# Making the sums of w_out's blocks on VectorE alone, through three buffers in turn

## The chip, the core and the metric

The kernel runs on one core of one Trainium2 chip. Its time is the device time of one execution in microseconds (us). TensorE does the matmuls, VectorE (DVE), ScalarE (ACT) and GpSimd (POOL) the elementwise work, SyncE (SP) issues the transfers. Each engine works through its own list of instructions in the order in which the program holds them, and waits on semaphores for the others.

## What is computed

The reference is a chain of three parts over 2304 tokens: attention with a bias made by a small network from relative positions, a gated block, and a block with squared ReLU. The change lies in the last:

```python
def _moe2_ref(x, w_in, w_out):          # x 2304x512, w_in 512x2048, w_out 2048x512
    h = np.maximum(x @ w_in, 0.0)
    return (h * h @ w_out).astype(np.float32)
```

## The kernel before

Every f32 matrix product is made of three f16 ones: each operand is split into a high half and a low half (the rest), and high x high, high x low and low x high are summed in PSUM. `parts2` makes such a split: a cast for the high half (L1198 on VectorE, L1200 on ScalarE) and a subtraction for the low half (`diff`, L1193, on VectorE or GpSimd). Which engine takes which is set by the table `MIX`: each letter has a cycle of engines (0 VectorE, 1 GpSimd or ScalarE), and `mixed` takes the next one at each call.

The last block runs over nine units of 256 tokens. The first is taken alone, by `plain(0)`: for each f of 0 to 7, `layer1` makes two groups of 12 matmuls (L1375), ScalarE evacuates each (L1380, ReLU) and squares it (L1384) into `zx`, and `parts2` writes both halves of block f into a part of `wr`; then 96 matmuls (L1403) make the output, 48 for each half of the tokens, block after block. The other eight units are taken in four pairs. `hidden` does `layer1` for a pair and forms four sums and differences of quarters of the result on GpSimd (`zx<-zx`, L1193); `outputs` multiplies them in seven products instead of eight (a Winograd scheme, L1447), which needs the like sums of w_out's quarters on the other side. I call `plain(0)` the single unit and the four pairs the first to the last pair stage. PSUM for L1375 and L1403 comes from five buffers in turn.

Those sums of w_out's quarters are made once, by `combine(f)` for f of 0 to 7: three sums of 512 columns and four of 256, in f32, in the buffer `w2t` of 1024 columns, each from the last, and then one `parts2` of 1024 columns into `st["TS"][f]`. In the names of the trace these are `w2t<-w2r`, `w2t<-w2t,w2r` and `w2t<-w2r,w2t` for the sums, and `w2s`, `w2c`, `w2r` or `wr` `<-w2t` for the split. The seven sums take their engine from letter "t", (0, 0, 1): two on VectorE, one on GpSimd. `combine` for f of 0 to 2 is called in `weights2`, for 3 to 6 between the blocks of `plain`, and for 7 after them.

The engines' order isn't the order of the code: the program is built by a scheduler that models the engines' times and places each instruction when its inputs and its buffer are free by that model. So a sum that waits for the buffer `w2t` is placed later, among other work.

Of the kernel before, what the change touches and what calls it, by code (L numbers as in the profile page):

```python
# [10 lines left out]
F32 = mybir.dt.float32  # L11
# [13 lines left out]
P = 128  # L25
# [4 lines left out]
MIX = {  # L30
# [4 lines left out]
}  # L35

# [39 lines left out]
def tile_attention_moe(  # L76
# [25 lines left out]
    st = {}  # L102
# [3 lines left out]
    def keep(n=1):  # L106
        sc_n[0] += 1
        return res.tile([P, n], F32, name=f"keep{sc_n[0]}")
# [77 lines left out]
    def mul(out_, a, b, f=1.0):  # L186
        nc.vector.scalar_tensor_tensor(out=out_, in0=a, scalar=f, in1=b, op0=ALU.mult, op1=ALU.mult)
# [26 lines left out]
    def mixed(k):  # L214

        mix_n[k] = mix_n.get(k, -1) + 1
        return MIX[k][mix_n[k] % len(MIX[k])]
# [197 lines left out]
    def mm():  # L415
        return ps_mm.tile([P, 512], F32, tag="mm", name="mm", bufs=2)
# [775 lines left out]
    def diff(out_, a, b, how, op=ALU.subtract):  # L1192
        (nc.gpsimd if how else nc.vector).tensor_tensor(out=out_, in0=a, in1=b, op=op)  # L1193

    def parts2(hi, lo, x, hw, lw):
        how = mixed(hw)
        if how == 0:
            nc.vector.tensor_copy(hi, x)  # L1198
        elif how == 1:
            nc.scalar.copy(hi, x)  # L1200
        else:
            nc.gpsimd.tensor_scalar(
                out=hi, in0=x, scalar1=1.0, scalar2=0.0, op0=ALU.mult, op1=ALU.add)
        diff(lo, x, hi, mixed(lw))

    def combine(f):

        q = st["w2r"].t.rearrange("p a b -> p (a b)").bitcast(F16).rearrange("p (s c) -> p s c", c=256)
        t = st["w2t"]
        tv = t.rearrange("p (a b c) -> p a b c", a=2, b=2)  # L1210
        t1, t2, t3, t4 = [t[:, 256 * i:256 * i + 256] for i in range(4)]
        a, b = 4 * (W2 + f), 4 * (W2 + 8 + f)

        def right(l):
            return q[:, a + 2 * l + 1:b + 2 * l + 2:32, :]

        def left(l):
            return q[:, a + 2 * l:a + 2 * l + 2, :]

        t13 = tv[:, :, 0, :]  # L1220
        diff(t13, right(0), left(0), mixed("t"))
        diff(t13, t13, right(1), mixed("t"), ALU.add)
        diff(t13, t13, left(1), mixed("t"))
        for x, c, y in ((t2, b + 1, t1), (t4, b, t2)):
            diff(x, q[:, c], y, mixed("t"))
            diff(x, x, q[:, c + 2], mixed("t"), ALU.add)
        hi, lo = st["TS"][f]
        parts2(hi, lo, t, "c", "d")

    def yt_load(us):  # L1230
        n = 256 * len(us)
        yt = st["yt"][:, 0:8 * n].rearrange("p (l t) -> p l t", l=8)
        for i, u in enumerate(us):
            nc.sync.dma_start_transpose(out=yt[:, :, 256 * i:256 * i + 256], in_=y_d[u][:, :])

    def weights2():
        a_stack.close()
        w2p = ctx.enter_context(tc.tile_pool(name="w2p", bufs=2, side="right"))
        ps2 = ctx.enter_context(tc.tile_pool(name="ps2", bufs=5, space=PSUM))
        w2r = Ring(w2p.tile([P, 25, 512], F32, name="w2r", bufs=1), {  # L1240
            "w": lambda j, kc: (w2a, 4 * j + kc) if j < 2 else 4 * j - 8 + kc, "2": lambda j, kc: W2 + kc})
        st["w2p"], st["ps2"], st["w2r"] = w2p, ps2, w2r

        def mm2():
            return ps2.tile([P, 512], F32, tag="ph", name="mm2")

        w2s = w2p.tile([P, 3584], F32, name="w2s", bufs=1)
        sg2 = Stage(
            512, [w2s[:, 1024 * i:1024 * i + 1024].bitcast(I64) for i in range(3)],
            [w2s[:, 3072 + 256 * i:3328 + 256 * i].bitcast(BF16) for i in range(2)])  # L1250
        yield from first(w2r, {"w": w2i}, range(2, 4), block_rows, sg2, 3, mm2)
        kappa = []
        for j in range(4):
            kap = keep()
            mul(kap, st["iw", j], st["iw", j], KR)
            kappa.append(kap)
        yield from second(w2r, "2", NF2, w2o, kappa, sg2, 3, mm2, True)
        new = w2p.tile([P, 4096], F16, name="w2c", bufs=1)

        st["w2t"] = w2p.tile([P, 1024], F32, name="w2t", bufs=1)  # L1260
        w2h, wrh, w2sh = [t.rearrange("p a b -> p (a b)").bitcast(F16) for t in (
            w2r.t, wr.t, w2s.rearrange("p (a b) -> p a b", a=7))]
        rooms2 = [w2sh[:, 1024 * i:1024 * i + 1024] for i in range(7)] + [w2h[:, 1024 * 24:1024 * 25]] + [
            new[:, 1024 * i:1024 * i + 1024] for i in range(4)] + [
            wrh[:, 1024 * i:1024 * i + 1024] for i in (4, 5, 6, 36)]
        st["TS"] = [rooms2[2 * f:2 * f + 2] for f in range(8)]
        st["HS"] = [wrh[:, int(1024 * o):int(1024 * o) + 3584] for o in (7.5, 11, 15, 18.5, 22, 25.5, 29, 32.5)]
        st["yt"] = wrh[:, 0:4096]
        for f in range(3):
            if f == 1:  # L1270
                yield ("gv", 8)
                yt_load((0,))
            combine(f)
            yield 3.0
# [61 lines left out]
    w2p, ps2, w2r = st["w2p"], st["ps2"], st["w2r"]  # L1336

    def mm2():
        return ps2.tile([P, 512], F32, tag="ph", name="mm2")
# [5 lines left out]


    wk = ctx.enter_context(tc.tile_pool(name="wk", bufs=2, side="left"))
    fac = res.tile([P, 18], F32, name="fac")
    nc.vector.tensor_scalar(out=fac, in0=ftok, scalar1=st["G1"], scalar2=None, op0=ALU.mult)
    mul(fac, fac, fac)  # L1350
# [83 lines left out]
    def outputs(us):  # L1434
        n = 256 * len(us)
        nh = n // 2
        last_bank = mm2()
        for t in range(nh // P):
            banks = [mm2(), mm2(), mm2()] if t else [ma(), mm(), mm()]
            (p1, p2), (p6, p7), (p5, p3) = [[bk[:, 256 * i:256 * i + 256] for i in range(2)] for bk in banks]  # L1440
            p4 = last_bank[:, 256 * t:256 * t + 256]

            def product(po, a, b, fs=range(8)):
                for f in fs:
                    for k, (l, wl) in enumerate(((0, 0), (0, 1), (1, 0))):
                        o = nh * (a - 1 + 7 * l) + P * t
                        nc.tensor.matmul(  # L1447
                            po, HS[f][:, o:o + P], right_of(f, wl, b),
                            start=f == 0 and k == 0, stop=f == 7 and k == 2)

            def sums(name):
                return wk.tile([P, 256], F32, tag=name, name=name)

            def add(name, x, y):
                o = sums(name)
                nc.vector.tensor_tensor(out=o, in0=x, in1=y, op=ALU.add)
                return o

            def row(j, h, src, other):

                i = nh * (1 - h) + P * t
                u, tt = us[i // 256], i % 256 // P
                sc = fac[:, 2 * u + tt:2 * u + tt + 1]
                o = obs[h][:, 256 * j:256 * j + 256]
                nc.vector.tensor_tensor(out=o, in0=src, in1=other, op=ALU.add)
                nc.scalar.activation(o, o, AF.Copy, scale=sc)

            obs = [wk.tile([P, DM], F32, tag="ob", name="ob", bufs=3) for _ in range(2)]
            early_, late_ = (range(6), range(6, 8)) if t == 0 else (range(8), ())
            for fs in (early_, late_):  # L1470
                for po, a, b in ((p1, A11, B11), (p6, S2, T2), (p5, S1, T1)):
                    product(po, a, b, fs)
            c1 = sums("c1")
            nc.scalar.copy(c1, p1)
            u2 = add("u2", p6, c1)
            u4 = add("u4", p5, u2)
            product(p7, S3, T3)
            u3 = add("u3", p7, u2)
            row(1, 1, p5, u3)
            product(p2, A12, B21)  # L1480
            row(0, 0, p2, c1)
            product(p3, S4, B22)
            row(1, 0, p3, u4)
            product(p4, A22, T4)
            row(0, 1, p4, u3)
            for h in range(2):
                i = nh * (1 - h) + P * t
                for p0, np_, r0 in out_rows(us[i // 256], i % 256 // P):
                    nc.sync.dma_start(out[r0:r0 + np_, :], obs[h][p0:p0 + np_, :])
# [37 lines left out]
```

## Time and profile before

| | |
|---|---|
| three timed runs | 1247.25 us median, 1245.92 to 1251.09 |
| the profiled execution | 1241.6 us, span 1239.8 us |
| TensorE busy | 1099.7 us, 89% of the span |
| VectorE, ScalarE, GpSimd busy | 782.3, 669.9, 642.3 us |
| `plain(0)`, from its second group to its last matmul | 868.05 to 908.34 |
| first pair stage | 908.34 to 1001.18 |
| the other three | 1001.18 to 1079.30, 1157.42 and 1235.54 |

Times of rows are counted from the start of the span. A row of the order of time names an engine, a line, an operation, output<-input, shapes and a count; in brackets stands how long the engine stood idle ahead of it and what released it. The granted clock is a share of TensorE's full 2.4 GHz; 1.00 is all of it, and a mean in between mixes the two levels 1.2 and 2.4.

### The profile page before, as it was taken

Reading aid. Unit: us, or ns where it says so; the run is one execution under the profiler, and the core shown is the slowest. Engines: PE = TensorE matmul, PEld = TensorE weight load, DVE = VectorE, ACT = ScalarE, POOL = GpSimd, SP = SyncE. Lnnn points to the kernel's source line nnn. Section 1 sums busy time; section 2 is a strip of 40 time slices with the busy share of each in tenths; the row PEclk is TensorE's granted clock in tenths of the full one; section 3 lists DMA queues with packets and bytes.
Section 4 is the critical chain, followed back from the end, with each engine's and each line's share of the span. In section 5 each row is a group of like instructions: output and inputs, shape, how many; then the busy total and the mean of one; then the engine's idle time right before and its main releaser. Section 6 shows DMA issues by size and latency. Waiting matters only on the chain. (4 is left out here: it accounts for less than half of the span.)

```text
span 1239.8 us, 27146 instructions
## 1 busy us (share of the span) xinstructions
PE 1099.7 (89%) x10478; PEld 811.3 (65%) x10478; DVE 782.3 (63%) x1866; ACT 669.9 (54%) x1350; POOL 642.3 (52%) x811
## 2 busy tenths in 40 slices
PE   2587799998678889999997999979998899999998
PEld 2566788686467578686774767556743756848657
DVE  5989857887676666666565745884757335153361
ACT  3567767557566566566563543365635245163451
POOL 2433213279768697778694462235567236062360
PEclk9779799999879999999999999989999899999999
DMA  8957543219999999998989994650201101002001
GB/s 220 266 134 208 177 132 87 50 58 201 220 214 209 217 218 169 230 184 170 182 170 247 240 228 129 213 176 10 43 17 23 30 18 35 35 1 52 19 1 35
DMA packets 278078, 163.20 MB, mean 132 GB/s; under 512 B 233276, under 2 KB 246588, under 8 KB 277948
## 3 DMA queue, kind: packets, MB, share of 16 engines
q1 hardware_dynamic: 277948, 161.46, 55.9%
q8 instruction: 82, 1.34, 0.5%
q14 instruction: 48, 0.39, 0.1%
HBM read 92.13 MB, written 19.48 MB: 90 GB/s over the span
## 5 line engine op out<-in xcount | busy, mean ns | idle before, releaser
L458 PEld LDWEIGHTS <-wr 128*128 128x128 f16 x2592 | 253.4, 100 | 50.7 <-issue 14.9
L1193 POOL TENSOR_TENSOR zx<-zx 128x256 f32<-128x256 f32 x128 | 123.3, 974 | 150.1 <-ACT zx L1384 145.4
L458 PE MATMUL mm<-xT,wr 128*128 128x256 f16 x1536 | 185.5, 276 | 7.9 <-DVE yh L500 3.4
L220 POOL TENSOR_TENSOR pt<-s,pt 128x512 f16<-128x512 f32 x224 | 173.1, 796 | 30.4 <-ACT pt L836 27.8
L1447 PEld LDWEIGHTS <-wr 128*128 128x128 f16 x1344 | 132.1, 99 | 23.8 <-ACT wr L1200 3.5
L220 POOL TENSOR_TENSOR zx<-th,zx 128x256 f16<-128x256 f32 x108 | 82.5, 765 | 123.7 <-ACT zx L443 117.6
L481 PE MATMUL mm<-wr,zx 128*128 128x512 f16 x612 | 143.1, 381 | 1.5 <-DVE sc L828 1.1
L1193 DVE TENSOR_TENSOR wr<-zx,wr 128x768 f16<-128x768 f32 (+2 forms) x72 | 93.3, 1302 | 66.6 <-ACT wr L1200 65.6
L821 DVE CUSTOM_DVE_ANT_0 s<-qk,room 128x576 f32<-128x576 f32 x144 | 107.8, 749 | 40.8 <-PE qk L812 24.0
L829 ACT ACTIVATE s<-s,sc 128x576 f32<-128x576 f32 x112 | 85.6, 771 | 56.1 <-DVE sc L828 48.9
L458 PE MATMUL mm<-zx,wr 128*128 128x256 f16 x864 | 105.1, 279 | 2.8 <-DVE th L469 1.5
L1375 PE MATMUL mm<-wr,room 128*128 128x512 f16 (+1 forms) x480 | 101.3, 361 | 4.6 <-ACT zx L1380 4.5
L481 PEld LDWEIGHTS <-zx 128*128 128x128 f16 x648 | 60.3, 98 | 66.4 <-issue 3.5
L604 DVE TENSOR_TENSOR scrap<-scrap,room 128x1024 f16<-128x1024 f16 (+1 forms) x108 | 85.1, 801 | 24.3 <-PE ma L643 20.6
L1375 PE MATMUL mm<-wr,w2r 128*128 128x512 f16 (+1 forms) x480 | 100.0, 358 | 0.0
L620 POOL TENSOR_TENSOR scrap<-scrap 128x256 f32<-128x256 f32 (+1 forms) x90 | 64.1, 712 | 64.7 <-ACT scrap L619 56.5
L874 PE MATMUL av<-vp,pT 128*128 128x65 f16 (+3 forms) x1792 | 70.8, 197 | 26.9 <-DMA pT<-pt 23.9
L874 PEld LDWEIGHTS <-pT 128*128 128x128 f16 (+1 forms) x1792 | 61.7, 103 | 42.3 <-DMA pT<-pt 33.0
L1375 PEld LDWEIGHTS <-room 128*128 128x128 f16 x480 | 47.2, 98 | 52.1 <-issue 7.5
L643 PEld LDWEIGHTS <-scrap 128*128 128x128 f16 x1440 | 60.0, 105 | 27.5 <-issue 11.9
L1375 PEld LDWEIGHTS <-w2r 128*128 128x128 f16 x480 | 47.0, 98 | 46.6
L812 PE MATMUL qk<-kp,qT 128*128 128x288 f16 x384 | 64.1, 293 | 11.4 <-DMA kp<-kT_d 6.1
(273 smaller groups left out, 2093.3 us busy)
## 6 DMA issues: line engine op xcount, KB each, us to landing
kp<-kT_d SPq DMA_DIRECT2D x64, 288.0 KB, 3.3
vp<-v_d SPq DMA_DIRECT2D x48, 325.0 KB, 3.6
w2s<-in_moe_w_out_dram SPq DMA_DIRECT2D x16, 512.0 KB, 4.1
wr<-in_moe_w_gate_dram SPq DMA_DIRECT2D x24, 256.0 KB, 4.8
wst<-in_moe_w_out_dram SPq DMA_DIRECT2D x12, 512.0 KB, 3.6
wr<-in_moe_w_val_dram SPq DMA_DIRECT2D x24, 256.0 KB, 4.2
v_d<-vp SPq DMA_DIRECT2D x16, 325.0 KB, 2.9
y_d<-yh SPq DMA_DIRECT2D x18, 256.0 KB, 3.4
```

Of the source, the lines that this page charges most:

```text
L220: nc.gpsimd.tensor_tensor(out=out_, in0=x, in1=hi, op=ALU.subtract)
L458: nc.tensor.matmul(pg[:, 256 * gi:256 * gi + 256], wr.parts(key, f // 4, cc, wl, P * (f % 4), P), mov(xl, cc), start=k == 0, stop=k == 11)
L481: nc.tensor.matmul(po, zall[:, f, zl, P * t:P * t + P], wr.parts("o", 0, f, wl), start=k == 0, stop=k == 3 * NF1 - 1)
L604: nc.vector.tensor_tensor(out=m[:, :, ni * e:ni * e + ni], in0=block(kb, i0, ni), in1=th, op=ALU.is_gt)
L620: nc.gpsimd.tensor_tensor(out=tmp[r], in0=tmp[r], in1=xb, op=ALU.mult)
L812: nc.tensor.matmul(pq[:, j, 0:288], qT[:, 2 * (n % 4) + s, :], kts[0][:, js], start=s == 0, stop=s == 1)
L821: nc.vector.tensor_tensor_reduce(out=s.rearrange("p (a j) -> p a j", a=2), in0=pq[:, :, 0:288], in1=bias[:, n].rearrange("p (a j) -> p a j ...
L829: nc.scalar.activation(s, s, AF.Exp, bias=nm, scale=-1.0)
L874: nc.tensor.matmul(av[r, slot, 0:cn], pT[:, 5 * l + c, r], vs[e][c][:, c0:c0 + cn], start=m == 0, stop=m == 13)
L1193: (nc.gpsimd if how else nc.vector).tensor_tensor(out=out_, in0=a, in1=b, op=op)
L1375: nc.tensor.matmul(ph[:, :n], w2r.parts("w", g // 4, cc, wl, P * (g % 4), P), yt[:, 4 * yl + cc, :], start=m == 0, stop=m == 11)
L1447: nc.tensor.matmul(po, HS[f][:, o:o + P], right_of(f, wl, b), start=f == 0 and k == 0, stop=f == 7 and k == 2)
```

## The change

The letter "t" of the table becomes (0,), so that all seven sums of each `combine` go to VectorE. A tile `four` of 2048 columns is allocated in the pool `wk`, and its two halves are put ahead of `w2t` in a list; each `combine` takes the list's first buffer and puts it at the end. The three calls in `weights2` come before `four` exists and still share `w2t`; the calls 3 to 7 take `four`'s first half, its second, `w2t`, and the two halves again. `outputs` gave its sums (`c1`, `u2`, `u4`, `u3`) tiles of their own, two of each; they now lie in quarters of `four`, one half for each half of the tokens. The lines behind the new ones are three higher.

```diff
-    "t": (0, 0, 1), "c": (1,), "d": (0, 1, 1), ...
+    "t": (0,), "c": (1,), "d": (0, 1, 1), ...
...
     def combine(f):
...
-        t = st["w2t"]
+        t = st["w2t"][0]
+        st["w2t"].append(st["w2t"].pop(0))
...
-        st["w2t"] = w2p.tile([P, 1024], F32, name="w2t", bufs=1)
+        st["w2t"] = [w2p.tile([P, 1024], F32, name="w2t", bufs=1)]
...
     wk = ctx.enter_context(tc.tile_pool(name="wk", bufs=2, side="left"))
+    four = wk.tile([P, 2048], F32, name="four", bufs=1)
+    st["w2t"] = [four[:, 0:1024], four[:, 1024:2048]] + st["w2t"]
...
-            def sums(name):
-                return wk.tile([P, 256], F32, tag=name, name=name)
+            def sums(i):
+                return four[:, 1024 * (t % 2) + 256 * i:1024 * (t % 2) + 256 * i + 256]
...
-            c1 = sums("c1")
+            c1 = sums(0)
             nc.scalar.copy(c1, p1)
-            u2 = add("u2", p6, c1)
-            u4 = add("u4", p5, u2)
+            u2 = add(1, p6, c1)
+            u4 = add(2, p5, u2)
```

TensorE's and SP's orders are the same as before. On VectorE, the stretch around the last low halves of the single unit (`wr<-zx,wr 128x512`) reads before:

```order
L1198 CAST wr<-zx 128x512
L1193 TENSOR_TENSOR wr<-zx,wr 128x512
L1193 TENSOR_TENSOR w2t<-w2t,w2r 128x2x256 x2
L1193 TENSOR_TENSOR wr<-zx,wr 128x512
L1193 TENSOR_TENSOR w2t<-w2t,w2r 128x256
L1193 TENSOR_TENSOR w2t<-w2r,w2t 128x256
L1193 TENSOR_TENSOR wr<-zx,wr 128x512
```

and after, the last row being the eighth low half as in the piece above:

```order
L1193 TENSOR_TENSOR four<-w2r,four 128x256 x2
L1193 TENSOR_TENSOR wr<-zx,wr 128x512
L1193 TENSOR_TENSOR four<-four,w2r 128x256 x2
L1193 TENSOR_TENSOR wr<-zx,wr 128x512
L1193 TENSOR_TENSOR w2t<-w2r 128x2x256
L1193 TENSOR_TENSOR w2r<-four,w2s 128x1024
L1193 TENSOR_TENSOR w2t<-w2t,w2r 128x2x256
L1193 TENSOR_TENSOR four<-w2r 128x2x256
L1193 TENSOR_TENSOR w2t<-w2t,w2r 128x2x256
L1193 TENSOR_TENSOR wr<-zx,wr 128x512
```

The sums of the calls 3 and 4, and the first of call 6, have moved in front of that half; before, those of call 3 began behind it.

On ScalarE, in the first pair stage (L1380 evacuates a group of layer 1, L1384 squares it, L1200 casts), before:

```order
L1200 CAST wr<-zx 128x1024
L1380 ACTIVATE zx<-mm_13945 128x512
L1384 ACTIVATE zx<-zx 128x512
L1380 ACTIVATE zx<-mm_13968 128x512
L1384 ACTIVATE zx<-zx 128x512
L1200 CAST wr<-zx 128x1024
L1200 CAST wr<-w2t 128x1024
L1380 ACTIVATE zx<-mm_13983 128x512
L1384 ACTIVATE zx<-zx 128x512
```

and after, from the last cast of `combine` on:

```order
L1200 CAST wr<-four 128x1024 x2
L1200 CAST w2c<-w2t 128x1024
L1410 ACTIVATE ob<-mm_13763,fac 128x512
L1383 ACTIVATE zx<-mm_13817 128x512
L1387 ACTIVATE zx<-zx 128x512
L1383 ACTIVATE zx<-mm_13832 128x512
L1387 ACTIVATE zx<-zx 128x512
```

The casts of `combine` (`w2c<-w2t`, `wr<-four`) have all moved in front of the stage's first evacuation (L1383 of the new line numbers); before, three of them stood among its evacuations.

## Rows read from the trace of the kernel before

**Rows 1.** Stretches: single unit, then four pair stages (busy us per engine, clock).

```profile
core 0: us, PE busy (x) PEld busy (x) DVE busy (x) ACT busy (x) POOL busy (x), PEclk, DMA share, GB/s
868.05:908.34 40.29, 40.29 (x275) 26.82 (x274) 26.83 (x43) 21.10 (x47) 21.55 (x18) 1.00 0.17 40
908.34:1001.18 92.84, 82.86 (x529) 52.50 (x528) 48.13 (x52) 36.31 (x56) 46.05 (x43) 0.94 0.08 21
1001.18:1079.30 78.12, 78.12 (x530) 51.65 (x528) 31.41 (x35) 34.03 (x53) 30.33 (x32) 1.00 0.10 28
1079.30:1157.42 78.12, 78.12 (x530) 51.66 (x528) 31.73 (x35) 33.97 (x53) 30.65 (x32) 1.00 0.12 28
1157.42:1235.54 78.12, 78.12 (x530) 51.56 (x527) 32.25 (x36) 33.25 (x52) 30.24 (x32) 1.00 0.04 14
```

**Rows 2.** TensorE in order of time: start, us, instruction, [idle before <-releaser].

```profile
887.62 20.88 PE L1403 MATMUL mm<-w2r,wr 128*128 128x512 f16 x96
908.34 2.75 PE L1375 MATMUL mm<-wr,room 128*128 128x512 f16 x12
...
941.10 2.75 PE L1375 MATMUL mm<-wr,room 128*128 128x512 f16 x12 [1.31 <-ACT zx L1380]
...
949.68 4.14 PE L1375 MATMUL mm<-wr,room 128*128 128x512 f16 x12 [3.24 <-ACT zx L1380]
```

**Rows 3.** Waits between 845 and 1010: total us, times, longest.

```profile
POOL w2t L1193 <- DVE w2t L1193: 17.5, 14, 3.7
...
DVE w2t L1193 <- POOL w2t L1193: 15.0, 13, 4.6
```

**Rows 4.** ScalarE in order of time, in front of the gap at 949.68.

```profile
946.94 1.04 ACT L1200 CAST wr<-zx 128x1024 f16<-128x1024 f32 x1 [4.08 <-POOL zx L1193]
948.09 1.04 ACT L1200 CAST wr<-w2t 128x1024 f16<-128x1024 f32 x1
949.04 0.59 ACT L1380 ACTIVATE zx<-mm 128x512 f32<-128x512 f32 x1
```

**Rows 5.** Instructions that write or read `w2t`: ns min/median/max, first and last start.

```profile
L1193 DVE TENSOR_TENSOR w2t<-w2t,w2r x21: 424/691/1255, 864.8 to 947.2; 128x256 f32<-128x256 f32 x11, 128x512 f32<-128x512 f32 x10
L1193 POOL TENSOR_TENSOR w2t<-w2t,w2r x11: 669/1154/1677, 866.1 to 944.9; 128x512 f32<-128x512 f32 x6, 128x256 f32<-128x256 f32 x5
L1193 DVE TENSOR_TENSOR w2t<-w2r,w2t x11: 414/426/1367, 867.3 to 946.3; 128x256 f32<-128x256 f16 x11
...
L1193 DVE TENSOR_TENSOR w2r<-w2t,w2s x1: 1226/1226/1226, 903.3 to 903.3; 128x1024 f16<-128x1024 f32 x1
```

**Rows 6.** The stretch from the first sum to the eighth low half.

```profile
863.50:893.50 30.00, 30.00 (x228) 22.17 (x227) 24.38 (x39) 19.04 (x45) 18.50 (x15) 1.00 0.23 53
```

**Rows 7.** VectorE in that stretch by form: busy us, mean ns | idle before.

```profile
L1193 DVE TENSOR_TENSOR wr<-zx,wr 128x512 f16<-128x512 f32 x8 | 6.9, 869 | 2.2 <-ACT wr L1200 2.1
L1193 DVE TENSOR_TENSOR w2t<-w2t,w2r 128x512 f32<-128x512 f32 x4 | 3.3, 828 | 0.0
...
L1193 DVE TENSOR_TENSOR w2t<-w2r,w2t 128x256 f32<-128x256 f16 x4 | 2.6, 658 | 1.9 <-POOL w2t L1193 1.8
L1198 DVE CAST wr<-zx 128x512 f16<-128x512 f32 x2 | 2.2, 1106 | 0.0
```

**Rows 8.** VectorE in order of time.

```profile
863.50 0.68 DVE L1193 TENSOR_TENSOR w2t<-w2r 128x512 f32<-128x512 f16 x1
...
886.21 1.21 DVE L1193 TENSOR_TENSOR wr<-zx,wr 128x512 f16<-128x512 f32 x1 [2.06 <-ACT wr L1200]
...
892.82 0.69 DVE L1193 TENSOR_TENSOR wr<-zx,wr 128x512 f16<-128x512 f32 x1
...
1013.10 0.56 DVE L1198 CAST wr<-zx 128x768 f16<-128x768 f32 x1
```

**Rows 9.** GpSimd in order of time.

```profile
857.38 1.15 POOL L220 TENSOR_TENSOR w2r<-w2r 128x512 f16<-128x512 f32 x1 [1.52 <-ACT w2r L209]
858.63 0.69 POOL L197 TENSOR_SCALAR w2r<-w2r,keep 128x512 f16<-128x512 f32 x1
...
884.75 2.13 POOL L1193 TENSOR_TENSOR w2s<-w2t,w2s 128x1024 f16<-128x1024 f32 x1 [1.94 <-ACT w2s L1200]
```

More of the change, by code (lines that the diff above doesn't have):

```diff
@@ L1449, in product, with add @@
                             start=f == 0 and k == 0, stop=f == 7 and k == 2)
-            def sums(name):
-                return wk.tile([P, 256], F32, tag=name, name=name)
-            def add(name, x, y):
-                o = sums(name)
+            def sums(i):
+                return four[:, 1024 * (t % 2) + 256 * i:1024 * (t % 2) + 256 * i + 256]
+            def add(i, x, y):
+                o = sums(i)
                 nc.vector.tensor_tensor(out=o, in0=x, in1=y, op=ALU.add)
@@ L1472, in outputs @@
                     product(po, a, b, fs)
-            c1 = sums("c1")
+            c1 = sums(0)
             nc.scalar.copy(c1, p1)
-            u2 = add("u2", p6, c1)
-            u4 = add("u4", p5, u2)
+            u2 = add(1, p6, c1)
+            u4 = add(2, p5, u2)
             product(p7, S3, T3)
-            u3 = add("u3", p7, u2)
+            u3 = add(3, p7, u2)
             row(1, 1, p5, u3)
```

2 rows, old and new, of the table MIX are left out of this document.

## The prediction, made before the change was run

> **What bounds the kernel now.** I read the stretches first, then TensorE's own order of time, then the waits around the stage that the change touches. The last four stages are alike in work: each takes two units of 256 tokens through 16 layer-1 groups and 14 products. Three of them last 78.12 us each with TensorE busy throughout at a granted clock of 1.00; the first, from 908.34 to 1001.18, lasts 92.84 us with 82.86 us busy at a clock of 0.94 [rows 1]. The excess is 92.84 - 78.12 = 14.7 us: 10.0 us in which TensorE stood, and 4.7 us in which it ran slower. After 1001.18 TensorE has no gap to save, and before 863 nothing is changed, so this excess is what there is to win.
>
> The first stage is the one into which the sums of w_out's blocks (`combine`) run over. In TensorE's order [rows 2] the long gap is 3.24 us ahead of 949.68, laid to ScalarE's evacuation at L1380; the groups behind it take 4.14 us instead of 2.75. In ScalarE's queue that evacuation (949.04) stands directly behind the cast of a `combine` result, 948.09, and that one behind a cast at 946.94 that waited 4.08 us for GpSimd [rows 4]. GpSimd and VectorE in turn wait for each other inside `combine`: 14 waits of GpSimd on VectorE, 17.5 us, and 13 the other way, 15.0 us [rows 3], since the sums alternate between the two engines and all go through the one buffer `w2t`. Each hand-over holds up the `hidden` work queued behind it.
>
> **The change: what leaves the first stage.** Seven sums per `combine`, eight calls: 56. GpSimd made 18 of them (11 + 5 + 2 by form, the 11 in [rows 5]); now VectorE makes all. With two more buffers the scheduler no longer spreads the last calls over the first pair of units: by the order, VectorE's sums all stand ahead of its first cast of `hidden`, and ScalarE's and GpSimd's parts of them ahead of theirs. The queues of the first stage then hold what those of the last stage hold (the mix of engines for `parts2` starts at the same place in both), and TensorE's and SP's orders are word for word as before. So I take the first stage at 78.12 us: **-14.7 us**.
>
> **What it costs: VectorE in the single unit.** The sums now crowd in front of `plain`'s own work. TensorE's second layer starts at 887.62 and ends at 908.34, 96 matmuls [rows 2]; the 45th is the first to read the low half of the eighth block, at 887.62 + 44/96 x 20.72 = 897.1. Before, VectorE finished that half at 892.82 + 0.69 = 893.5 [rows 8], 3.6 us early. Counted in the order from the first sum (863.50) to that half, 16 sums of 512 columns stand on VectorE instead of 6, 16 of 256 instead of 8, and two low halves of 1024 instead of one: 10 x 0.69 + 8 x 0.43 + 1.23 = 11.5 us by their lone times [rows 5]. VectorE had 24.4 us busy in these 30 us [rows 6]; the other 5.6 us, waits for the other engines, I take as filled, since sums of two or three calls now stand ready between one another.
>
> Instructions of VectorE and GpSimd stretch each other: the subtraction at 886.21 took 1.21 us against 0.68, while GpSimd's at 884.75 ran until 886.88 [rows 8, 9]. Over the stretch, eight low halves at 869 ns, four sums at 828 and four at 658, and two casts at 1106 [rows 7] against 680, 690, 430 and 560 (the larger cast at 1013.10 [rows 8]) make 1.5 + 0.6 + 0.9 + 1.1 = 4.1 us of stretching within the 24.4. An instruction that follows another starts some 0.08 us before its end, 1.5 us for the 19 more. GpSimd keeps four subtractions of 1.15, three scalings of 0.69 and two low halves of 2.13 there, 10.9 us [rows 9]; its seven sums of the stretch are gone. Three values then follow:
> - no stretching: 24.4 - 4.1 + 11.5 - 1.5 = 30.3 us, done at 893.8, no wait of TensorE;
> - stretching as before: 34.4 us, done at 897.9, a wait of 0.8 us;
> - VectorE pays for all of GpSimd's 10.9 us: 41.2 us, done at 904.7, a wait of 7.6 us.
>
> I take 36.5 us, a third of the way from the second to the third: GpSimd has less work there than before, but it meets a VectorE that never idles, so that it can't be less than the second. Done at 900.0: a wait of **+2.9 us** in front of the 45th matmul. Then the clock: a gap of 1.31 us left the next group at its 2.75 us, one of 3.24 us cost the next group 4.14 - 2.75 = 1.4 us [rows 2]. For a gap of 2.9 I take half, **+0.7 us**, with 0 and 1.4 as ends.
>
> **What else moves.** The sixth call's sums end VectorE's list. Behind the eighth low half stand 8 sums of 512 columns, 16 of 256 and one low half of 1024, 13.6 us alone and some 16 with GpSimd's last low halves between, so they end near 916; ScalarE's cast of them stands ahead of the evacuation of the first group of the stage, which TensorE gives out at 911.1 plus the wait. The five PSUM buffers let TensorE run on, and the low halves, casts and subtractions of the stage fill VectorE 31 to 32 us, ScalarE 33 to 34 and GpSimd 30 to 31 of 78 [rows 1], so that a lag of 2 to 4 us can be made up in the 41 us of layer 1. I cost it at nothing; if it isn't made up, 1 us. The first write to the new buffers waits until the last y block of the stage before has left the region; its store is issued before VectorE arrives, and I cost that at nothing too (at most 1 us, VectorE's queue behind it). The output sums now sit in quarters of the same two buffers, in the same order and twice over as before: nothing. No DMA is added, and no queue of SP is passed.
>
> **Sum.** -14.7 + 2.9 + 0.7 = -11.1 us. The profiled execution took 1241.6 us (span 1239.8), which would become 1230.5; the median of the three timed runs is 1247.25, 5.6 us above it, and I see no reason for the difference to change. Forecast: 1247.25 - 11.1 = **1236 us**.
>
> **The rivals.**
> 1. VectorE is in time, as with less stretching: the whole 14.7 us are won, 1232.5. For it: GpSimd's queue there is nearly empty between 883 and 911, and the longest calls lie in it. Against: two of GpSimd's low halves fall before the deadline.
> 2. The two engines exclude each other wholly: a wait of 7.6 us, 1.4 of clock and 1 of lag are given back, -4.7 us, 1242.5. For it: the stretched subtraction ended 0.54 us after GpSimd's end, which looks like waiting out the other's instruction rather than sharing [rows 8, 9]. Against: before, VectorE paid some 4 us beside GpSimd's 18.5 us busy [rows 6]. The Trainium skill (SBUF — State Buffer, section "SBUF: two separate sides") says that a VectorE instruction with two SBUF inputs and a GpSimd instruction take an exclusive lock on a shared pair of ports, and the loser blocks for the whole instruction. That row agrees with it; its full consequence would be this rival.
> 3. The first stage stays slow: with the sums gone, the next thing late is `hidden`'s own chain (evacuate, square, four GpSimd sums, cast, low half), 1247. For it: GpSimd had 46.05 us busy there. Against: the last stage has the same chain in the same mix and no gap [rows 1].
> 4. Slower: VectorE becomes the bound of the single unit. If every one of the 32 sums ahead of the eighth half took the longest time seen, 1.26 and 1.37 us [rows 5], that is 16 x 0.57 + 16 x 0.94 = 24.1 us over the lone sum of 30.3; done at 917.9, TensorE waits 20.8 us, with 1.4 of clock, against 14.7: +7.5, 1255. It decides from 897.1 + 14.7 = 911.8 on. Against: GpSimd has not 24 us of work there to collide with.
>
> That the buffers aren't used in turn would be a fifth; the order shows `four` and `w2t` written between each other, so I give it nothing.
>
> **How the numbers follow.** Forecast 0.45, rival 1 0.17, rival 2 0.23, rival 3 0.08, rival 4 0.07. 0.5% is 6.2 us, about what a measurement can tell from no change: faster means under 1241.0. That is the forecast, rival 1 and, with its ends between 1237 and 1243, rather more than half of rival 2, with 0.03 off for scatter: 0.78; within 0.5%: the rest of rival 2 and rival 3, 0.15; slower: 0.07. The range takes in rival 1, less 2.5 us for the runs' own spread (lowest run 1.3 under the median, the profiled one 5.6 under), and rival 2 up to its value: 1230 to 1242.5, which leaves out rivals 3 and 4 and the edges.
>
> **What would show it.** The stage behind the single unit should last 78 us at a clock of 1.00, with no gap ahead of L1447's first products. TensorE should show one gap inside its 96 second-layer matmuls, near 897, released by VectorE, of 1 to 5 us. The eighth low half should end near 900. GpSimd's sums of `w2t` should be gone, with VectorE's near 0.43 and 0.69 us after 883. I am wrong if the first stage keeps gaps ahead of its evacuations, or if VectorE reaches that half after 905.

## The result and the profile after

The changed kernel takes 1233.95 us (median), against 1246.63 us for the kernel before beside it: a ratio of 0.9871, 95% interval 0.9833 to 0.9910. In a second set of runs on another occasion it was 1234.86 against 1245.78 us, 0.9914 (0.9888 to 0.9941). One of the first set's six executions of the changed kernel was slow (1460.30 us at a granted clock of 0.72); its median counts it, the ratio doesn't, and the other five have a median of 1232.17 us. The kernel is faster, by 11 to 13 us between the medians; forecast was 11.1 us and 1236 us, with a range of 1230 to 1242.5.

The profiled execution took 1225.56 us with a span of 1223.8, 16.0 us under the span of before. Not all of that belongs to the change. I count from the single unit's second group (the ten matmuls of layer 1 right behind the last ones of L481) to the end of the last pair stage, and call this **the stretch**. Before, it ran from 868.05 to 1235.54, 367.49 us. The windows of the changed kernel answer [rows 1]; columns as there:

```profile
core 0: us, PE busy (x) PEld busy (x) DVE busy (x) ACT busy (x) POOL busy (x), PEclk, DMA share, GB/s
863.35:905.76 42.41, 40.51 (x275) 26.72 (x274) 41.86 (x72) 23.91 (x50) 14.64 (x9) 1.00 0.16 38
905.76:985.14 79.38, 78.64 (x529) 51.43 (x528) 36.62 (x41) 33.50 (x53) 34.88 (x34) 1.00 0.09 24
985.14:1063.26 78.12, 78.12 (x530) 51.65 (x528) 31.39 (x35) 34.05 (x53) 30.28 (x32) 1.00 0.13 28
...
sum 356.15, PE 353.50 PEld 233.02 DVE 173.83 ACT 158.68 POOL 140.61; mean PE 70.70 PEld 46.60 DVE 34.77 ACT 31.74 POOL 28.12
```

The first pair stage fell from 92.84 to 79.38 us and its clock rose from 0.94 to 1.00; the single unit grew from 40.29 to 42.41; the other three stages stayed at 78.12. That is -13.46 + 2.12 = -11.34 us. The remaining 4.7 us of the profiled difference lie ahead of the stretch: up to the first sum of `combine`, 4.5 us ahead of it, both programs hold the same instructions in the same order.

TensorE in order of time, the rows that answer [rows 2]:

```profile
879.35 1.47 PE L1378 MATMUL mm<-wr,w2r 128*128 128x256 f16 x12 [0.31 <-ACT zx L1383]
...
883.27 9.66 PE L1406 MATMUL mm<-w2r,wr 128*128 128x512 f16 x44
894.53 11.40 PE L1406 MATMUL mm<-w2r,wr 128*128 128x512 f16 x52 [1.59 <-DVE wr L1193]
...
955.16 0.94 PE L1450 MATMUL mm<-wr 128*128 128x256 f16 x7 [0.70 <-DVE wr L1198]
```

The gaps of 1.31 and 3.24 us ahead of layer-1 groups are gone. A new one of 1.59 us stands in front of the 45th of the 96 matmuls, released by VectorE's eighth low half. A last one, 0.70 us, stands in the first pair stage's products. Why the half is late is in VectorE's own order, which answers [rows 8], and in GpSimd's, which answers [rows 9]:

```profile
858.81 0.68 DVE L1193 TENSOR_TENSOR w2t<-w2r 128x512 f32<-128x512 f16 x1
...
886.20 2.20 DVE L1193 TENSOR_TENSOR wr<-zx,wr 128x512 f16<-128x512 f32 x1 [0.34 <-ACT wr L1200]
...
888.92 3.15 DVE L1193 TENSOR_TENSOR w2r<-four,w2s 128x1024 f16<-128x1024 f32 x1
...
893.79 0.68 DVE L1193 TENSOR_TENSOR wr<-zx,wr 128x512 f16<-128x512 f32 x1
```

```profile
884.73 3.12 POOL L1193 TENSOR_TENSOR w2s<-w2t,w2s 128x1024 f16<-128x1024 f32 x1 [9.54 <-ACT w2s L1200]
888.44 2.54 POOL L1193 TENSOR_TENSOR w2c<-four,w2c 128x1024 f16<-128x1024 f32 x1 [0.59 <-ACT w2c L1200]
```

The subtraction of 0.68 us at 886.20 took 2.20 and ended at 888.40, 0.55 us after GpSimd's low half (887.85). The low half of 1.22 us at 888.92 took 3.15 and ended 1.09 us after GpSimd's next one (890.98). Without these two delays, 1.5 and 1.9 us, the eighth half, which ended at 894.47, would have been ready in front of the matmul that needs it (892.9).

### The profile page after: what moved, and what is told of

Read it like the earlier page. It is cut to its first block, busy times and chain, and to the rows that moved or that the text cites. A ratio compares the mean times of both kernels' runs of the same rounds, so it can differ in the third digit from the quotient of the medians.

```text
span 1223.8 us, 27145 instructions
## 1 busy us (share of the span) xinstructions
PE 1091.4 (89%) x10478; PEld 807.8 (66%) x10478; DVE 789.5 (65%) x1884; ACT 670.6 (55%) x1350; POOL 621.1 (51%) x793
## 4 chain that ended last, share of the span: by engine, by line
PE 44%; DMA 18%; DVE 15%; POOL 10%; ACT 6%; issue 5%; SPq 2%; POOLq 0%; ACTq 0%; DVEq 0%
PE mm L458 11%; PE mm L1378 10%; PE mm L1450 10%; DMA pT<-pt 5%; POOL pt L220 3%; PE mm L481 3%; POOL zx L1193 2%; PE av L874 2%; DMA wr<-in_v_dram 2%; DMA qT<-qs 2%; PE qk L812 2%; PE ma L1450 1%; DVE w2t L1193 1%; DMA w2s<-in_moe_w_out_dram 1%; DVE scrap L604 1%
## 5 line engine op out<-in xcount | busy, mean ns | idle before, releaser
L481 PE MATMUL mm<-wr,zx 128*128 128x512 f16 x612 | 142.1, 379 | 1.6 <-DVE th L469 1.6
L1193 DVE TENSOR_TENSOR wr<-zx,wr 128x768 f16<-128x768 f32 (+1 forms) x72 | 93.6, 1307 | 71.4 <-ACT wr L1200 70.4
L481 PEld LDWEIGHTS <-zx 128*128 128x128 f16 x648 | 60.1, 98 | 66.1 <-issue 2.8
L1469 ACT ACTIVATE ob<-ob,fac 128x256 f32<-128x256 f32 x32 | 16.0, 507 | 104.0 <-DVE ob L1468 103.9
```

The costliest lines, as they stand in the source:

```text
L481: nc.tensor.matmul(po, zall[:, f, zl, P * t:P * t + P], wr.parts("o", 0, f, wl), start=k == 0, stop=k == 3 * NF1 - 1)
```

## The experiments

All are compared by the stretch of one profiled execution, since what lies ahead of it varies from one execution to the next (below), and by the ratio of the timed runs to the kernel before beside them (its medians there were 1245.74 to 1247.61 us, so a median of the table is compared through its ratio). Where TensorE never waits, the stretch is 40.15 + 4 x 78.12 = 352.6 us. The last three stages took 78.12 us each before and after, so the move of the output sums into `four` cost nothing.

| kernel | single unit | first stage | stretch | median | ratio (95%) |
|---|---|---|---|---|---|
| before | 40.29 | 92.84 | 367.49 | 1245.74 | 1 |
| before, again | 40.28 | 92.21 | 366.84 | | |
| the change | 42.41 | 79.38 | 356.15 | 1233.95 | 0.9871 (0.9833 to 0.9910) |
| the change, again | 42.53 | 79.37 | 356.26 | 1234.86 | 0.9914 (0.9888 to 0.9941) |
| VectorE alone, one buffer | 40.15 | 89.66 | 364.17 | 1241.48 | 0.9962 (0.9940 to 0.9984) |
| three buffers, engines mixed | 50.17 | 78.72 | 363.24 | 1240.94 | 0.9959 (0.9936 to 0.9982) |
| VectorE alone, two buffers | 40.16 | 84.81 | 359.33 | 1239.27 | 0.9947 (0.9921 to 0.9974) |
| GpSimd alone, three buffers | 40.18 | 96.00 | 370.54 | 1252.64 | 1.0067 (1.0023 to 1.0112) |
| before, low halves on VectorE | 40.27 | 90.46 | 365.09 | 1242.83 | 0.9979 (0.9951 to 1.0006) |
| the change, low halves on VectorE | 40.62 | 78.12 | 353.10 | 1233.25 | 0.9897 (0.9868 to 0.9925) |
| the same, again | 40.16 | 78.37 | 352.89 | 1234.59 | 0.9903 (0.9870 to 0.9937) |
| the change, two sums of seven | 46.96 | 78.12 | 359.43 | 1235.93 | 0.9928 (0.9902 to 0.9954) |
| that, low halves on VectorE | 45.93 | 78.12 | 358.41 | one run | |

### How firm one profile is

The changed kernel again:

> The changed kernel once more, profiled anew. The stretch is counted from the single unit's second group (the ten layer-1 matmuls right behind the last matmuls of L481) to the end of the last pair stage: 367.5 us before, 356.2 in the first profile of the changed kernel, 352.8 if TensorE never waits. If the wait behind VectorE's eighth low half is a property of the order and of the collisions with GpSimd's low halves, the stretch is again 355 to 358 with one gap of 1 to 3 us in the 96 matmuls. If it was an accident of that one execution, the gap is under 0.5 and the stretch 353 to 354. What lies ahead of the stretch differed by 13 us between the profiled executions and is expected to differ again; the ratio to before should stay between 0.985 and 0.991.

The kernel before again:

> The kernel before once more, for a second profile. The changed kernel's two profiles had the same stretch, 356.2 and 356.3 us, though they reached it 15 us apart. If the stretch of the kernel before is as fixed, it is 367.5 again within 1 us, with the first pair stage at 92 to 94; if it depends on when the stretch is reached, it differs by several us, and the 11.3 us between the two kernels were partly chance.

The changed kernel reached its stretch 15.1 us later than in its first profile (878.43 for 863.35) and took 356.26 us for it, 0.1 more. The kernel before took 366.84, 0.65 less. So the stretch can be read from one profile, and the span can't: the spans of the second profiles, 1239.0 and 1241.4, differ by only 2.4 us. The gap in front of the 45th matmul is back too, 2.21 us, but it came about in another way. GpSimd and VectorE in the second profile:

```profile
888.98 11.97 POOL L220 TENSOR_TENSOR w2r<-w2r 128x512 f16<-128x512 f32 x1 [2.85 <-ACT w2r L209]
900.91 2.58 POOL L1193 TENSOR_TENSOR w2s<-w2t,w2s 128x1024 f16<-128x1024 f32 x1
```

```profile
899.18 0.75 DVE L1193 TENSOR_TENSOR four<-four,w2r 128x256 f32<-128x256 f32 x2
900.28 1.23 DVE L1193 TENSOR_TENSOR wr<-zx,wr 128x512 f16<-128x512 f32 x1 [0.34 <-ACT wr L1200]
903.53 2.60 DVE L1193 TENSOR_TENSOR w2t<-w2r 128x512 f32<-128x512 f16 x1 [2.02 <-POOL w2s L1193]
```

GpSimd's subtraction of 1.15 us took 11.97: from 889.74 to 899.93 VectorE ran 23 instructions without a pause, at their lone times, and GpSimd finished 1.02 us after the start of VectorE's first pause, which lasted 0.34. Its low half then came late, and VectorE waited 2.02 us for that, to write the buffer again.

### The engine or the buffers

VectorE alone through the one buffer; the diff is against the kernel before:

```diff
-    "t": (0, 0, 1), "c": (1,), "d": (0, 1, 1), ...
+    "t": (0,), "c": (1,), "d": (0, 1, 1), ...
```

> Half of the change: all seven sums on VectorE, but through the one buffer w2t as before. I measure the stretch from the single unit's second group (the start of its TensorE work behind L481) to the end of the last pair stage: 367.5 us before, 356.2 with the whole change, 352.8 if nothing stood. With one buffer each call must wait until the cast (1.04 us) and the low half (1.2 or 2.1 us) of the call before are done, some 3 us eight times, and by the order two casts of combine still stand among the first stage's evacuations. My theory (the crossing of engines and the one buffer each hold the calls up) expects a stretch of 359 to 362, a first stage of 80 to 84 us. If the engine alone did it: 356. If the buffers alone did it: 367.

The stretch was 364.17 and the first stage 89.66, both over what I expected. VectorE no longer waits for GpSimd's sums, but each call waits until the low half of the call ahead has read the buffer:

```profile
908.62 0.69 DVE L1193 TENSOR_TENSOR w2t<-w2r 128x512 f32<-128x512 f16 x1
...
915.91 0.69 DVE L1193 TENSOR_TENSOR w2t<-w2r 128x512 f32<-128x512 f16 x1 [3.31 <-POOL w2c L1193]
...
923.22 1.20 DVE L1193 TENSOR_TENSOR w2t<-w2r 128x512 f32<-128x512 f16 x1 [3.32 <-POOL w2c L1193]
```

From call to call it takes 7.3 us (sums, ScalarE's cast, GpSimd's low half), so the last calls still lie in the first pair stage. In ScalarE's order the cast of the last one stands in front of an evacuation, as in [rows 4], but TensorE doesn't wait for that one here. GpSimd makes the low half of that cast (945.41) ahead of `hidden`'s own sums, and the products that need `hidden`'s parts come late: TensorE's five gaps of the stage, 7.9 us, all stand among the products, the longest behind a cast of `hidden`.

```profile
944.28 1.04 ACT L1200 CAST wr<-w2t 128x1024 f16<-128x1024 f32 x1 [1.89 <-DVE w2t L1193]
945.24 0.59 ACT L1380 ACTIVATE zx<-mm 128x512 f32<-128x512 f32 x1
```

```profile
945.41 2.13 POOL L1193 TENSOR_TENSOR wr<-w2t,wr 128x1024 f16<-128x1024 f32 x1 [3.23 <-ACT wr L1200]
```

```profile
970.09 0.39 PE L1447 MATMUL ma<-w2r,wr 128*128 128x256 f16 x2 [3.80 <-ACT wr L1200]
```

Three buffers, with the sums on both engines; the diff is against the changed kernel:

```diff
-    "t": (0,), "c": (1,), "d": (0, 1, 1), ...
+    "t": (0, 0, 1), "c": (1,), "d": (0, 1, 1), ...
```

> The other half: three buffers in turn, but the sums alternate between VectorE and GpSimd as before. By the order all casts of combine stand ahead of the first stage's first evacuation. If getting the calls done ahead of the first stage is what counts, the stretch (367.5 before, 356.2 with the whole change) comes out at 354 to 359, the first stage at 78 to 80 us, and the wait inside the single unit's 96 matmuls is no longer than the 1.6 us of the whole change, since VectorE has fewer sums. If the crossing between the engines is what counts, the waits of GpSimd on VectorE and back stay above 20 us together and the stretch stays at 362 or more.

The rival was right: 363.24 us. The first pair stage is free (78.72), and the waits between the engines now fall in the single unit, 50.17 us: TensorE stood 7.3 us in it, 4.1 of them among the 96 matmuls, and its clock there was 0.97. Waits of that kernel from 865 to 925 (total us, times, longest):

```profile
DVE w2t L1193 <- POOL w2t L1193: 7.8, 4, 5.2
POOL w2t L1193 <- DVE w2t L1193: 6.7, 7, 1.8
POOL four L1193 <- DVE four L1193: 6.4, 6, 3.1
...
PE mm L1406 <- DVE wr L1193: 3.5, 3, 2.2
```

So the engine alone is worth 3.3 us of the stretch, the buffers alone 4.3, and both together 11.3. Either half leaves a chain that is longer than its place: through one buffer, or from engine to engine.

Two buffers in turn instead of three:

```diff
-    st["w2t"] = [four[:, 0:1024], four[:, 1024:2048]] + st["w2t"]
+    st["w2t"] = [four[:, 0:1024]] + st["w2t"]
```

> The changed kernel with two buffers in turn (the first half of the new tile and the old buffer) instead of three. A call's sums, its cast on ScalarE and its low half on GpSimd took 7.3 us from call to call with one buffer (sums from 908.62, 915.91 and 923.22), 3.5 us of it the sums, so two buffers cover the rest for calls that follow one another. If two are enough, the stretch is 354 to 358 like the changed kernel's 356.2, with the gap of 1 to 3 us in the 96 matmuls. If the third is needed, the calls run over into the first pair stage again and the stretch is 359 to 364.

359.33 us: the third buffer is needed, for 3.2 of the 11.3 us. The single unit has no gap (40.16); the first pair stage has 84.81. The last cast of `combine` comes 9.7 us after its start (919.47) instead of 4.6 with three buffers, and TensorE has this row in it:

```profile
960.88 0.39 PE L1450 MATMUL ma<-w2r,wr 128*128 128x256 f16 x2 [3.23 <-ACT wr L1200]
```

GpSimd in VectorE's place, with three buffers:

```diff
-    "t": (0,), "c": (1,), "d": (0, 1, 1), ...
+    "t": (1,), "c": (1,), "d": (0, 1, 1), ...
```

> Three buffers, and all seven sums on GpSimd instead of VectorE: again no sum waits for the other engine. If what counts is only that one engine makes them all, the stretch is 354 to 358 as with VectorE. If what counts too is how long the one engine takes (GpSimd's sums took 1.15 and 0.67 us alone against 0.69 and 0.43, and it makes low halves of 2.13), its list for eight calls is some 60 us against the 50 from the first sum to the end of the single unit, three casts are left among the first pair stage's evacuations, and the stretch is 358 to 366, most of the excess in that stage.

370.54 us, beyond what I expected, and slower than before in the timed runs too. One engine for all sums isn't enough; it must get them done in the single unit, and GpSimd, which is slower at them and has `hidden`'s sums and the low halves besides, doesn't. Which of the two counts for more was not separated. The windows, single unit and first pair stage:

```profile
870.42:910.60 40.18, 40.18 (x275) 26.79 (x274) 21.86 (x24) 21.69 (x47) 36.91 (x36) 1.00 0.17 40
910.60:1006.60 96.00, 84.57 (x529) 52.94 (x528) 37.81 (x36) 36.74 (x56) 63.14 (x61) 0.93 0.07 20
```

GpSimd is full in the single unit (36.91 of 40.18 us) and carries the rest over, 63.14 us busy in the stage instead of 34.88.

### What the new wait is made of

The change with all low halves of `combine` on VectorE:

```diff
-    "t": (0,), "c": (1,), "d": (0, 1, 1), ...
+    "t": (0,), "c": (1,), "d": (0,), ...
```

> The whole change, and the low halves of combine on VectorE too (letter d (0,) for (0, 1, 1)), so that GpSimd has nothing of combine left and can't stretch VectorE's sums. In the whole change two instructions of VectorE that met GpSimd's low halves ahead of the eighth low half took 2.20 and 3.15 us for 0.68 and 1.22, 3.4 us over; two low halves of 1.2 us each, some 2.3 with overlap, take their place. So the eighth low half comes 1.1 us earlier and the wait of 1.6 us shrinks to about 0.5; behind it 3.7 us of stretching go and 3.5 us of low halves come. The first stage should lose its last 1.3 us. Stretch 353 to 354.5 (356.2 with the change). If the stretching were only the instructions' own cost, VectorE would be later by 2.3 us and the wait would grow to 4.

> The changed kernel with all low halves of the sums of w_out's blocks on VectorE too, once more, with more rounds. Its first profile had a stretch of 353.1 us, 3.0 below the changed kernel's, but its median was only 0.7 below. If the 3 us are real and the rest is what lies ahead of the stretch, the stretch is again 353 to 354.5 and the median 2 to 4 us below that of the changed kernel run beside it. If VectorE's longer list costs something that the one profile missed, the stretch is 355 or more and the medians are equal.

The stretch was 353.10 and 352.89 us, next to its floor: VectorE has more instructions, and the wait is gone. In the first profile TensorE runs its 96 matmuls in one piece:

```profile
896.49 20.88 PE L1406 MATMUL mm<-w2r,wr 128*128 128x512 f16 x96
```

```profile
872.02 0.68 DVE L1193 TENSOR_TENSOR w2t<-w2r 128x512 f32<-128x512 f16 x1
...
904.80 0.68 DVE L1193 TENSOR_TENSOR wr<-zx,wr 128x512 f16<-128x512 f32 x1
```

The eighth half now ends 33.5 us after the first sum, 2.2 us sooner. Of these, 0.6 us are the order's: one sum that stood ahead of the half now stands behind it. The rest is the stretching that went, less the low halves that came. So the gap of 1.6 to 2.2 us in the changed kernel and the lag behind it come mainly from GpSimd's low halves, not from VectorE's list of sums.

The 3.0 to 3.4 us of the stretch hardly show in the medians: in the second set this kernel's was 0.3 us below that of the change (1234.59 against 1234.86), where I expected 2 to 4. The timed runs of the changed kernel spread over 15 us, more than enough to cover 3; whether something ahead of the stretch takes them back stays open.

The same on the kernel before:

```diff
-    "t": (0, 0, 1), "c": (1,), "d": (0, 1, 1), ...
+    "t": (0, 0, 1), "c": (1,), "d": (0,), ...
```

> The kernel before (one buffer, two sums on VectorE and one on GpSimd) with all low halves of the sums on VectorE. If the hand-overs of the sums through the one buffer hold up the first pair stage, it keeps them: the stretch is 364 to 368 against 367.5, the first pair stage 89 to 93 us. If GpSimd's low halves were what held it up before, as they are what is left in the changed kernel, the stretch falls to 355 to 360.

365.09 us, the first pair stage 90.46. The hand-overs keep most of the excess: moving the low halves takes off 2.4 us here (1.8 against the second profile of before), which the timed runs can't tell from no change.

Two sums of seven, as a measure of what the sums cost:

```diff
-        diff(t13, right(0), left(0), mixed("t"))
-        diff(t13, t13, right(1), mixed("t"), ALU.add)
-        diff(t13, t13, left(1), mixed("t"))
-        for x, c, y in ((t2, b + 1, t1), (t4, b, t2)):
-            diff(x, q[:, c], y, mixed("t"))
-            diff(x, x, q[:, c + 2], mixed("t"), ALU.add)
+        diff(t13, right(0), left(0), 0)
+        diff(tv[:, :, 1, :], right(0), left(0), 0)
```

> The cost of the sums taken away: of the seven sums of each combine only the first difference is made, twice, so that the buffer is written; the other sums are left out and the casts and low halves stay. This gives the floor of what a better placing of the sums can bring. I expect no wait in the single unit and a first stage of 78.1 us: a stretch of 352.8 to 353.5, against 356.2 with the whole change and 367.5 before. If the first stage were slow for a cause of its own, its excess would stay: a stretch over 360.

It failed: 359.43 us, 3.3 more than with all seven sums. Since it had two gaps behind ScalarE's evacuations, I took GpSimd's low halves for the cause and moved them:

> Leaves out five of the seven sums of each block of w_out (the first difference is made twice), so the weights of the products are other numbers; and all low halves of the result go to VectorE. With GpSimd's low halves in place the same short list had a stretch of 359.4 us, 6.6 above the floor of 352.8, all of it in the single unit, with gaps of 2.7 and 1.9 us behind ScalarE's evacuations. If GpSimd's low halves cause those gaps, by holding up VectorE's sums for which ScalarE's casts wait ahead of the evacuations, the stretch is 352.8 to 353.8. If the casts' place in ScalarE's queue alone causes them, it stays at 357 to 360.

That failed too: 358.41. TensorE and ScalarE there:

```profile
890.97 1.73 PE L1374 MATMUL mm<-wr,w2r 128*128 128x256 f16 x12 [3.95 <-ACT zx L1379]
```

```profile
889.59 1.05 ACT L1200 CAST w2c<-w2t 128x1024 f16<-128x1024 f32 x1 [3.63 <-DVE w2t L1193]
890.54 1.20 ACT L1379 ACTIVATE zx<-mm 128x256 f32<-128x256 f32 x4
```

With short calls the order puts all eight casts of `combine` ahead of the single unit's last evacuations; with all seven sums four of them stand behind. One of these casts waited 3.63 us for VectorE, and four evacuations stood behind it. VectorE itself came late in part because it had kept GpSimd out: a subtraction of 1.15 us on GpSimd took 5.76, and VectorE's queue then waited 1.84 us for the scaling behind it.

```profile
877.45 5.76 POOL L220 TENSOR_TENSOR w2r<-w2r 128x512 f16<-128x512 f32 x1 [2.69 <-ACT w2r L209]
```

```profile
884.03 0.75 DVE L191 SCALAR_TENSOR_TENSOR w2r<-w2r,keep 128x512 f16<-128x512 f32 x1 [1.84 <-POOL w2r L197]
```

These two kernels therefore don't measure the sums: leaving work out moved the casts, and the first pair stage (78.12 in both) is all that they confirm.

## Why the prediction was right, and where it wasn't

**What bounds the kernel: right, by a path of which the prediction followed half.** The excess of the first pair stage went as named: GpSimd has no sums left, the waits of `w2t` between the engines are gone, and the gaps behind ScalarE's evacuations with them. But those two gaps were 4.55 of the 10.0 us in which TensorE stood. The other 5.4 us stood among the products, where the longest gap is as long as the one of [rows 2]. They have the same source: GpSimd makes the low half of the cast of [rows 4] ahead of `hidden`'s sums, whose casts the products need. The kernel before:

```profile
966.97 0.61 PE L1447 MATMUL ma<-w2r,wr 128*128 128x256 f16 x2 [3.21 <-ACT wr L1200]
```

```profile
949.27 2.13 POOL L1193 TENSOR_TENSOR wr<-w2t,wr 128x1024 f16<-128x1024 f32 x1 [1.50 <-ACT wr L1200]
951.36 8.39 POOL L1193 TENSOR_TENSOR zx<-zx 128x256 f32<-128x256 f32 x8
```

The prediction's sentence that each hand-over holds up the `hidden` work behind it covers this, and since it took the whole excess, its sum does too.

**-14.7 us for the first stage: 1.3 too much.** It fell by 13.46. I had seen the lag with which the stage begins and costed it at nothing, or 1 us if it isn't made up. ScalarE's order in the changed kernel:

```profile
910.31 1.04 ACT L1200 CAST w2c<-w2t 128x1024 f16<-128x1024 f32 x1 [5.79 <-DVE w2t L1193]
911.26 0.68 ACT L1410 ACTIVATE ob<-mm,fac 128x512 f32<-128x512 f32 x1
911.84 0.59 ACT L1383 ACTIVATE zx<-mm 128x512 f32<-128x512 f32 x1
```

TensorE had finished that group by 908.5, so the first evacuation came 3.3 us late (forecast: a lag of 2 to 4). Layer 1 made up most of it; 0.70 us remained as the gap at 955.16, and TensorE's rows were 0.5 us longer in total. In the kernel with all low halves on VectorE the stage took 78.12 and 78.37.

**+2.9 us for the wait: 0.8 too much, in its parts by offsetting errors.** The eighth half ended 35.7 us after the first sum (894.47 - 858.81), and 35.8 in the second profile; forecast was 36.5. My 36.5 was 30.3 of lone work and 6.2 of stretching. Measured, the stretched rows before the half add up to some 7.2 us, which leaves 28.5 for the rest; that the two errors nearly cancel is luck. TensorE came to the 45th matmul 34.1 us after the first sum instead of 33.6, so the gap was 1.59 us. The single unit grew by 2.12 us, since it has another gap of 0.31 ahead of 879.35 and 0.2 us of longer rows; in the second profile it grew by 2.2, nearly all of it the gap of 2.21.

**+0.7 us for the clock: nothing came.** The matmuls behind the gap of 1.59 ran at a granted clock of 1.00, and so did those behind the 2.21 of the second profile. What the term rested on was one execution. In [rows 2] the gap of 3.24 us was followed by a single group of 4.14 us (clock 0.64; the group behind it took 2.75 again, so the prediction's "groups" is one group), and the same gap in the second profile of the kernel before by one at the full 2.75. Nor did the slow group cost the stage its 1.4 us. First profile:

```profile
959.22 0.28 PE L1447 MATMUL ma<-w2r,wr 128*128 128x256 f16 x1 [0.96 <-DVE wr L1193]
```

Second profile:

```profile
951.88 2.75 PE L1375 MATMUL mm<-wr,room 128*128 128x512 f16 x12 [3.23 <-ACT zx L1380]
...
961.42 0.28 PE L1447 MATMUL ma<-w2r,wr 128*128 128x256 f16 x1 [2.35 <-DVE wr L1193]
```

Both reach this product 9.54 us after the start of that group: where the group was quick, TensorE waited 1.4 us longer for VectorE's low half. So the prediction's split of the excess, 10.0 us of standing and 4.7 of slower running, isn't fixed either: it was 11.6 and 2.5 in the second profile, in a stage of nearly the same length.

**The sum** of -11.1 stands beside -11.3 and -10.6 (first profiles, second profiles). That is nearer than its terms are: a stage 1.3 us less improved, and a wait with its clock 1.5 us cheaper, cancel by luck.

**The rivals.** Rival 1 (no wait) and rival 2 (7.6 us of wait) bracket what came. Rival 2's mechanism is what the rows show: VectorE's two blocked instructions ended 0.55 and 1.09 us after GpSimd's, each 0.13 us short of its lone time. The Trainium skill (SBUF — State Buffer, section "SBUF: two separate sides") has the engine that comes second blocked for the other's whole instruction; the trace agrees for VectorE, whose blocked subtraction took 2.20 us for 0.68. Only the price failed: it let VectorE pay for all of GpSimd's work, while GpSimd paid too, 11.97 us for 1.15 in one execution. Rival 3 didn't come: with the sums gone from the stage, a gap of 0.70 us is left in it, which is gone where the low halves of `combine` are moved too. Rival 4 found no support: VectorE was busy 41.86 of 42.41 us, yet its half came 35.7 us after the first sum and not 54.

## What to carry to other kernels

A chain that runs from engine to engine through one buffer has two causes of length, and taking away one moves the wait instead of ending it: here 3.3 and 4.3 us alone, 11.3 together. When work is moved to an engine that then never idles, ask which instructions of the neighbour it collides with; moving those as well took another 3 us off the stretch here, though the timed runs didn't show it. A gap ahead of one group can be only part of a delay that shows again further on, so follow the whole queue. Leaving work out is no measure of its cost where a scheduler places the rest anew; compare the orders first.

## What the runs showed of the hardware

VectorE can keep GpSimd out for far longer than one instruction. In the second profile of the change with all low halves on VectorE, GpSimd's subtraction of 1.15 us took 14.30 us (888.08 to 902.38); in the first profile of the same kernel it took 1.25. Which of the two pays isn't fixed by the order: in the first profile of the changed kernel this subtraction took 1.24 us, and the two sums of VectorE beside it took 2.24 instead of 1.28. That the 14.30 us are no fault of the record shows in VectorE, which in the end had to wait for it:

```profile
888.08 14.30 POOL L220 TENSOR_TENSOR w2r<-w2r 128x512 f16<-128x512 f32 x1 [2.85 <-ACT w2r L209]
```

```profile
900.69 0.68 DVE L1193 TENSOR_TENSOR w2t<-w2r 128x512 f32<-128x512 f16 x1
902.41 1.23 DVE L1193 TENSOR_TENSOR w2r<-four,w2s 128x1024 f16<-128x1024 f32 x1 [1.05 <-POOL w2r L220]
```

It ended 1.0 us after VectorE's queue had stopped at 901.37, so that it began, in effect, only then. In the case of 11.97 us it was a row of 23 instructions without a pause that kept GpSimd out.

What a gap costs in clock varied: behind 3.23 us the next group ran at a granted clock of 1.00, behind 3.24 us it took 1.4 us longer at 0.64, and with GpSimd alone a gap of 2.11 us ahead of 941.37 was followed by a group of 4.44 us instead of 2.75, at 0.60.

The time ahead of the stretch differed by up to 15 us between profiled executions of programs that are alike there (starts at 863.35 to 878.43), in many steps of 1 to 2 us spread over that time. What causes them was not examined.
